# The last 96 feed-forward features computed token-major and turned by DMA, in one transformer block

## The chip, the cores and the metric

The kernel runs on one core of one Trainium2 chip. The time is the device time of a run in microseconds (us). A ratio is the mean time of one kernel's fast runs over the mean of the fast runs of the kernel before in the same rounds, so it is not quite the ratio of the medians that are quoted. "Span" is the time from the first to the last instruction in a trace. It is about 1.8 us shorter than the device time of the same run.

In profile lines PE is TensorE, PEld its loads of stationary tiles, DVE is VectorE, ACT is ScalarE, POOL is GpSimd, SP is SyncE, which here only issues DMAs; a "q" after the name means the engine's sequencer. L903 is line 903 of that kernel.

## The reference, cut to what matters

```python
h = _layernorm(x) * (1 + ca) + sa
x = x + ga * attention(h)              # 32 heads of 16, a softmax feature map, linear attention
h = _layernorm(x) * (1 + cb) + sb
g = silu(h @ w_gate); u = h @ w_up     # (2048, 512) @ (512, 1376)
x = x + gb * ((g * u) @ w_down)        # (2048, 1376) @ (1376, 512)
```

1376 features are 10 blocks of 128 and one, block 10, of 96.

## The kernel before

The program is recorded as operations with their engine alternatives. A long list, `ORDER`, made offline, says in which order a small planner takes them; the planner gives buffers and PSUM banks and so fixes each engine's instruction order. Attention for the next tokens and the feed-forward of the last ones are interleaved in it.

```python
UNITS = [(0, 0, 1), (0, 1, 1), (0, 2, 1), (0, 3, 1), (1, 0, 2), (1, 2, 2), ...]  # chunk, first tile, tiles (6 units have 2)
...
def ffn_gu(unit, ms, guT):                       # some feature blocks ms of one unit
    ...
    def f(ps_, wt):                              # features stationary, tokens moving: the result is feature-major
        for q, m in enumerate(ms):
            for k in range(KD):
                nc.tensor.matmul(ps_()[0:fsz, q * n:(q + 1) * n], lhsT=wt[:, k, m * P:m * P + fsz], rhs=h2[k], ...)
    pl.op("PE", ..., fn=lambda: f(g, wg_sb))     # gate, its own bank (L903)
    pl.op("PE", ..., fn=lambda: f(u, wu_sb))     # up, its own bank (L903)
    ...                                          # ACT: silu (L910); DVE: multiply (L913), or ACT copy + POOL multiply (L917, L919)
def ffn_down(unit, t, guT):                      # gu stationary, w_down moving (L949)
    ...
for ms in [... blocks 0 to 9 ...] + [[FM - 1]]:  # FM - 1 = 10, the block of 96, is its own group
    ffn_gu(unit, ms, guT)
```

Ones are multiplied on TensorE in some of its gaps ("fillers", L1015); their results aren't used.

The softmax here doesn't subtract the row's maximum and nothing guards it: scores larger than these inputs give would overflow.

## Time and profile before

| | before |
|---|---|
| device time, median of 3 runs | 211.17 us (210.75 to 211.92) |
| span of the trace | 208.8 us |
| TensorE clock granted | recorded as full throughout (but in the first 4 us matmuls of 512 columns start 427 ns apart, later 216 ns) |
| start of the last `phik` accumulation (end of stage one) | 56.27 us |
| start of the last matmul (end of stage two) | 205.46 us |
| fillers and idle gaps of TensorE in stage two | 0.65 and 0.59 us |

The two times in the middle cut the run into a stage that GpSimd paces and one that TensorE paces. They are read from the starts of single matmuls in the trace. The difference, 149.19 us, is the length of stage two. The page, the chain and the matmul groups are in the prediction.

### The profile page before, as it was taken

Reading aid. Unit: us, or ns where it says so; the run is one execution under the profiler, and the core shown is the slowest. Engines: PE = TensorE matmul, PEld = TensorE weight load, DVE = VectorE, ACT = ScalarE, POOL = GpSimd, SP = SyncE. Lnnn points to the kernel's source line nnn. Section 1 sums busy time; section 2 is a strip of 40 time slices with the busy share of each in tenths; the row PEclk is TensorE's granted clock in tenths of the full one; section 3 lists DMA queues with packets and bytes.
Section 4 is the critical chain, followed back from the end, with each engine's and each line's share of the span. In section 5 each row is a group of like instructions: output and inputs, shape, how many; then the busy total and the mean of one; then the engine's idle time right before and its main releaser. Section 6 shows DMA issues by size and latency. Waiting matters only on the chain.

```text
span 208.8 us, 4769 instructions
## 1 busy us (share of the span) xinstructions
PE 201.6 (97%) x1802; PEld 140.3 (67%) x1825; DVE 141.7 (68%) x337; ACT 115.3 (55%) x244; POOL 133.3 (64%) x175
## 2 busy tenths in 40 slices
PE   7899999999999999999999999999999999999994
PEld 2665564545556689779857866886875888846973
DVE  6698998999467896898789876884823431335224
ACT  2798999999798965325324721345424435410530
POOL 3358999899950558939648995587377737362230
PEclk9999999999999999999999999999999999999999
DMA  5999994994000012141311223212320010022001
GB/s 177 344 386 115 347 177 81 389 384 137 3 0 0 3 27 54 29 51 25 79 25 28 75 52 82 48 25 53 101 52 0 28 50 25 16 64 75 3 25 50
DMA packets 31465, 19.24 MB, mean 92 GB/s; under 512 B 22513, under 2 KB 28114, under 8 KB 31442
## 3 DMA queue, kind: packets, MB, share of 16 engines
q1 hardware_dynamic: 31152, 18.85, 33.6%
q8 instruction: 14, 0.23, 0.4%
q10 hardware_dynamic: 290, 0.08, 0.2%
q14 instruction: 9, 0.07, 0.1%
HBM read 11.58 MB, written 2.10 MB: 66 GB/s over the span
## 4 chain that ended last, share of the span: by engine, by line
PE 82%; ACT 8%; POOL 4%; DMA 2%; issue 2%; SPq 1%; DVE 0%; ACTq 0%
PE one_ps L903 37%; PE one_ps L949 18%; PE one_ps L849 6%; PE one_ps L670 4%; POOL phik L639 4%; PE four_ps L778 4%; PE one_ps L614 3%; ACT e L621 3%; PE one_ps L610 3%; DMA wqkv_sb<-in_A_wqkv_dram 2%; PE kv_ps L1015 2%; ACT hT L581 2%; ACT eT L676 2%; PE one_ps L444 1%; PE one_ps L489 1%
## 5 line engine op out<-in xcount | busy, mean ns | idle before, releaser
L910 ACT ACTIVATE sg<-one_ps 128x512 bf16<-128x512 f32 (+3 forms) x52 | 26.1, 528 | 46.8 <-PE one_ps L903 45.4
L903 PE MATMUL one_ps<-hT,wu_sb 128*128 128x256 bf16 (+3 forms) x440 | 45.2, 251 | 0.1
L903 PE MATMUL one_ps<-hT,wg_sb 128*128 128x256 bf16 (+3 forms) x440 | 44.8, 251 | 0.1
L903 PEld LDWEIGHTS <-wu_sb 128*128 128x128 bf16 (+1 forms) x440 | 36.8, 100 | 6.1
L949 PE MATMUL one_ps<-wd_sb,gu 128*128 128x512 bf16 (+2 forms) x168 | 40.0, 372 | 0.4
L903 PEld LDWEIGHTS <-wg_sb 128*128 128x128 bf16 (+1 forms) x440 | 36.8, 100 | 4.7 <-issue 0.2
L913 DVE TENSOR_TENSOR gu<-one_ps,sg 128x512 bf16<-128x512 f32 (+2 forms) x30 | 17.8, 596 | 24.8 <-PE one_ps L903 21.3
L919 POOL TENSOR_TENSOR gu<-usb,sg 128x512 bf16<-128x512 bf16 (+1 forms) x22 | 22.3, 1020 | 18.6 <-ACT usb L917 10.2
L639 POOL TENSOR_TENSOR phik<-e,R 128x1024 bf16<-128x1024 bf16 x16 | 30.6, 1928 | 1.6 <-ACT eT L676 0.7
L949 PEld LDWEIGHTS <-gu 128*128 128x128 bf16 (+1 forms) x187 | 17.9, 98 | 15.5
L917 ACT CAST usb<-one_ps 128x512 bf16<-128x512 f32 (+1 forms) x22 | 11.5, 523 | 21.4 <-PE one_ps L903 21.4
L381 DVE BATCH_NORM_STATS2 st<-x_c 128x6 f32<-128x512 bf16 x32 | 21.3, 681 | 1.5 <-DMA x_c<-in_A_x_dram 1.3
L836 POOL TENSOR_TENSOR o<-o 128x512 bf16<-128x512 bf16 x14 | 16.1, 1151 | 7.5 <-DVE o L816 7.5
L816 DVE TENSOR_TENSOR o<-four_ps,A 128x512 bf16<-128x512 f32 x32 | 20.6, 684 | 0.0
L631 DVE TENSOR_REDUCE S<-e 128x64 f32<-128x1024 bf16 x16 | 19.2, 1199 | 1.3 <-ACT e L621 1.0
L960 DVE TENSOR_TENSOR fg<-one_ps,gab 128x512 bf16<-128x512 f32 (+1 forms) x16 | 10.6, 672 | 12.0 <-PE one_ps L949 9.3
L676 ACT ACTIVATE eT<-one_ps 128x512 bf16<-128x512 f32 x32 | 17.7, 640 | 1.5 <-PE one_ps L670 1.4
L852 DVE TENSOR_TENSOR x_c<-x_c,one_ps 128x512 bf16<-128x512 bf16 x16 | 11.0, 685 | 10.5 <-PE one_ps L849 10.3
L621 ACT ACTIVATE e<-one_ps 128x512 bf16<-128x512 f32 x32 | 17.8, 638 | 0.0
L610 PE MATMUL one_ps<-Wk,hT 128*128 128x512 bf16 x63 | 16.3, 379 | 0.4 <-ACT hT L581 0.2
L849 PE MATMUL one_ps<-wo_sb,oT 128*128 128x512 bf16 x58 | 16.1, 379 | 0.3
L670 PE MATMUL one_ps<-hT,Wq 128*128 128x512 bf16 x62 | 15.3, 379 | 0.1
(109 smaller groups left out, 287.1 us busy)
## 6 DMA issues: line engine op xcount, KB each, us to landing
wmod_sb<-in_w_mod_dram SPq DMA_DIRECT2D x2, 1024.0 KB, 7.5
out_dram<-ot SPq DMA_DIRECT2D x15, 128.0 KB, 2.1
wg_sb<-in_B_w_gate_dram SPq DMA_DIRECT2D x1, 1376.0 KB, 8.3
wu_sb<-in_B_w_up_dram SPq DMA_DIRECT2D x1, 1376.0 KB, 11.3
wd_sb<-in_B_w_down_dram SPq DMA_DIRECT2D x1, 1280.0 KB, 14.3
x_c<-in_A_x_dram SPq DMA_DIRECT2D x4, 256.0 KB, 4.7
wmod_sb<-in_w_mod_dram SPq DMA_DIRECT2D x4, 256.0 KB, 5.3
wqkv_sb<-in_A_wqkv_dram SPq DMA_DIRECT2D x2, 512.0 KB, 6.8
```

What stands on the lines that cost most here:

```text
L381: pl.op("DVE", r=reads, w=[st6], us=0.6, fn=lambda: nc.vector.bn_stats(st6()[:], src))
L610: nc.tensor.matmul(pk()[:], lhsT=hT[c_i][k][:, cols], rhs=Wk2[:, k, :], start=(k == 0), stop=(k == KD - 1))
L621: nc.scalar.activation(e()[:, :, sg].rearrange("p g h f -> p g (h f)"), pk()[:].rearrange("p (g n) -> p g n", g=G), ACT.Exp, scale=(1.0, - ...
L639: pl.op("POOL", r=[e, R], w=[bphik[i]], us=1.92, fn=lambda: nc.gpsimd.tensor_tensor(bphik[i]()[:].rearrange("p g s h f -> p (g s h) f"), e ...
L670: nc.tensor.matmul(pq()[:], lhsT=Wq2[:, k, j * P:(j + 1) * P], rhs=hT[c_i][k][:], start=(k == 0), stop=(k == KD - 1))
L676: pl.op("ACT", r=[pq, btab], w=[beT[c_i, sg, j]], us=0.48, fn=lambda sg=sg: nc.scalar.activation(eTs[c_i, sg, j][:], pq()[:], ACT.Exp, sca ...
L816: nc.vector.tensor_tensor(o2()[:, sg].rearrange("p j (h d) -> p j h d", d=DH), ndv()[:, :, sg, 0:P].rearrange("p j (h d) -> p j h d", d=DH ...
L849: nc.tensor.matmul(a()[:], lhsT=oT()[:, j, :], rhs=wo_sb[:, j, :], start=(j == 0), stop=(j == KD - 1))
L903: nc.tensor.matmul(ps_()[0:fsz, q * n:(q + 1) * n], lhsT=wt[:, k, m * P:m * P + fsz], rhs=h2[k], start=(k == 0), stop=(k == KD - 1))
L910: pl.op("ACT", r=[g, btab], w=[sg], us=0.08 + 0.41 * L / CW, fn=lambda: nc.scalar.activation(sg()[0:fsz, 0:L], g()[0:fsz, 0:L], ACT.Silu))
L919: pl.op("POOL", r=[usb, sg], w=[gu], us=0.17 + 0.98 * L / CW, fn=lambda: nc.gpsimd.tensor_tensor(gu()[0:fsz, 0:L], usb()[0:fsz, 0:L], sg() ...
L949: nc.tensor.matmul(fp()[:], lhsT=b()[0:fsz, c0:c0 + P], rhs=wd_[0:fsz, m, wcs], start=(m == 0), stop=(m == FM - 1))
```

## The change

Block 10 costs TensorE as much as a full block when its 96 features are the stationary side. The change makes the 128 tokens stationary and moves the 96 features past them, so that only 96 columns are paid. The result is then token-major; the down projection needs it feature-major, so each token tile's block goes through a DMA transpose. `ORDER` was made anew.

```diff
+    def ffn_tail(unit, guT):
+        c_i, t0, w = unit
+        cs = slice((FM - 1) * P, F)
+        gu = sb("qf", "gu", [P, CW], BF16)
+        for q in range(w):
+            ps_ = bank("gu", (P, 2 * lastf))
+            ...
+                for i, wt in enumerate((wg_sb, wu_sb)):
+                    for k in range(KD):
+                        nc.tensor.matmul(ps_()[:, i * lastf:(i + 1) * lastf], lhsT=hT[c_i][k][:, toks], rhs=wt[:, k, cs], ...)
+            ...  # ACT: silu of the gate half into sgl; DVE: up half times sgl into gul[:, 0:96]
+            pl.op("XBAR", r=[gul], w=..., fn=... nc.sync.dma_start(
+                gu()[:, q * P:(q + 1) * P], gul()[:], transpose=True))
...
-        for ms in [...] + [[FM - 1]]:
+        ffn_tail(unit, guT)
+        for ms in [...]:
             ffn_gu(unit, ms, guT)
```

Cut: the new `ORDER`, four gul tiles of 128x128 whose last 32 columns are zeroed once on GpSimd, and the down projection's dependence on the turn of its own tile.

## The prediction

> **What bounds the kernel now.** I read the views in the order whole page, chain, matmul groups by shape, timeline. From the page come these lines:
>
> ```profile
> span 208.8 us, 4769 instructions
> ...
> PE 201.6 (97%) x1802; PEld 140.3 (67%) x1825; DVE 141.7 (68%) x337; ACT 115.3 (55%) x244; POOL 133.3 (64%) x175
> ...
> PEclk9999999999999999999999999999999999999999
> ...
> PE 82%; ACT 8%; POOL 4%; DMA 2%; issue 2%; SPq 1%; DVE 0%; ACTq 0%
> ```
>
> TensorE is busy nearly throughout at its full clock, and 82% of the chain that ended last is its. But busy is not the same as bound: up to about 56 us it also multiplies a tile of ones to fill gaps, and these count as busy. So I ask the chain, in order of time, where one limit gives way to another. It starts (from 33 us) with ScalarE and GpSimd:
>
> ```profile
> 51.69 0.47 issue
> 52.16 1.33 POOL phik L639
> 53.50 0.55 issue
> 54.05 1.94 POOL phik L639
> 56.03 0.43 PE kv_ps L646 x8
> ...
> 98.17 2.23 PE one_ps L903 x40
> ...
> 163.48 17.47 PE one_ps L903 x160
> ...
> 182.69 8.65 PE one_ps L949 x40
> ```
>
> The reader is to see two stages. The first, to about 56.3 us, ends when GpSimd has made the 16th `phik` (16 times 1.93 us, almost back to back from 18.8 us in the timeline). Its last accumulation on TensorE starts at 56.27 us. After that nearly every piece is TensorE's own. I checked this by summing 1/2.4 ns per moving column plus 2.5 ns over every matmul that the program has after that point: 148.6 us, of which 0.65 us is filler. From 56.27 us to the last matmul's end at 205.65 us is 149.4 us. So the second stage has only some 0.7 us in which TensorE does nothing, nearly all between 68.8 and 72 us where the feed-forward starts (a gap of 0.25 and one of 0.28 us; gaps of just 0.216 us elsewhere are records missing from the trace). In this stage, less work on TensorE means an earlier end, one for one.
>
> The changed work, the last 96 features (block 10 of 11), is in that stage, by shape:
>
> ```profile
> L903 PE MATMUL one_ps<-hT,wu_sb 128*96 128x256 bf16 x24 | 3.6, 273 | 0.0
> L903 PE MATMUL one_ps<-hT,wg_sb 128*96 128x256 bf16 x24 | 3.6, 272 | 0.0
> L903 PE MATMUL one_ps<-hT,wg_sb 128*96 128x128 bf16 x16 | 1.7, 219 | 0.1
> L903 PE MATMUL one_ps<-hT,wu_sb 128*96 128x128 bf16 x16 | 1.5, 219 | 0.1
> ```
>
> The 272 ns are a matmul's whole latency. What counts is the distance of starts. From the timeline and the chain:
>
> ```profile
> 161.15 0.60 PE L903 MATMUL one_ps<-hT,wu_sb 128*96 128x256 bf16 x4
> 161.58 0.60 PE L903 MATMUL one_ps<-hT,wg_sb 128*96 128x256 bf16 x4
> 162.02 1.25 PE L949 MATMUL one_ps<-wd_sb,gu 128*128 128x512 bf16 x5
> ...
> 85.43 0.45 PE one_ps L903 x8
> ...
> 88.06 0.50 PE four_ps L778 x8
> ...
> 26.30 0.26 PE kv_ps L646 x8
> ```
>
> Starts at 161.15, 161.58 and 162.02 us: four matmuls of 256 columns per 0.435 us, 109 ns each. Eight of 128 columns take 0.45 us (56 ns), eight of 144 take 0.50 us (62.5 ns), eight of 65 take 0.26 us (33 ns). A stationary of only 96 columns makes none of them faster: block 10 costs as much as a full block of 128 features. That is the waste which the change goes for.
>
> **What the Trainium skill says.** "TensorE: Matmul & The Clock Gate", section "Back-to-back issue gap", gives N/2.4 + 2.5 ns for a warm gap. The trace agrees at 256, 144 and 128 columns (109.2, 62.5 and 55.8 ns by the formula) and is 3 ns above it at 65 (29.6 ns). Section "LDWEIGHTS (loading the stationary operand)" of that page puts a load at P/1.2, 107 ns for 128 columns. The trace shows 98 ns for 128 columns, 123 ns for 96. But the starts are 33 ns apart with 128-column loads in the 65-column stream, so loads overlap and don't set the pace there. "DMA: Bandwidth & Descriptors", section "Rules for kernel authors", wants transposes from different queues serialized. Here all are issued from SP, before and after, so no such wait is added. The same page's section "Anatomy of one DMA — SWDGE (gpsimd) path" fits some 2.0 us of fixed cost (for another queue kind). The trace has 2.3 to 2.4 us from issue to landing of a transpose.
>
> **The change part by part.** *Removed from TensorE:* the first four units hold one token tile (8 matmuls of 128 columns), the other six hold two (8 of 256). 4 x 8 x 56 ns + 6 x 8 x 109 ns = 1.79 + 5.23 = 7.02 us.
>
> *Added to TensorE:* 16 token tiles x 8 matmuls with 128 tokens stationary and 96 features moving. No row has 96 columns. The points at 128 and 65 bracket it, and 96/2.4 + 2.5 gives 42.5 ns. I take 43 ns, an estimate from the formula and the 33 ns seen at 65. 128 x 43 ns = 5.5 us. The loads rise from 80 to 128, which costs nothing if they stay hidden. The work falls by 7.02 - 5.5 = 1.5 us. The changed program's own order of matmuls agrees: after the last accumulation it has 146.4 us without fillers, by the same sum, against 148.0.
>
> *ScalarE:* removed are 4 x 0.260, 6 x 0.376 and 6 copies x 0.361 = 5.5 us. Added are 16 silus of 96 columns, 0.23 us each (along the line through 260 ns at 128 columns and 376 at 256) = 3.7 us. *VectorE:* 4 x 0.277 us removed, 16 x 0.24 us added, +2.8 us, which lies beside TensorE: VectorE is busy 38.8 of the 45 us from 72 to 117 us and less after. *GpSimd:* six multiplications of 0.67 us go; four small memsets of about 0.13 us come early. None of these is on the second stage's path.
>
> *SP queue:* 16 more transposes. The path from a tail's last matmul to the turned block is latency of the matmul 0.2 + silu 0.23 + multiply 0.24 + transpose 2.4 + hops, say 4 to 5 us. In the changed order the closest reader (the down projection) comes 8.5 us of TensorE work after its tail, most 10 to 25 us. So it is hidden, unless SP stands behind an earlier issue.
>
> *Moved:* the whole order of the program was made anew, and this is the part that I can't read off a row. Comparing the two orders: the last `phik` of stage one still has 16 products and six normalizations in one GpSimd row ahead of it, so its length should stay. But VectorE now takes two Wk copies (0.69 us each) in place of two hT evictions (0.34 us each) just before the statistics of tiles 4 to 7, some 0.6 us later; part of that is lost in the waits that GpSimd has there today (0.6 us at 21.3 us). I book +0.2 us. At the start of the feed-forward there are four fillers instead of three, so the gap is a little longer: +0.2 us. The end (last matmul, an addition of 0.42 us, two stores) has the same form in both.
>
> Sum: 211.17 - 1.5 + 0.2 + 0.2 = 210.1. A new order made for the new program may as well have found something, so I shade it to 209.9 us.
>
> **The rivals.** (1) *The loads set the pace.* With 128 loads of 98 ns laid end to end the tail would cost 12.5 us, +5.5 us: 216.7 us. Against it stands the 65-column stream at 33 ns with the same loads. If a load's floor were 56 ns, the tail would cost 7.2 us, and the time would stay at 211.4. (2) *The turned block comes late.* SP issues in order, and it already waits up to 23.6 us for one GpSimd product; an oT transpose behind a waiting tail would delay attention. Each late one costs what exceeds the 8.5 us slack; two or three of 1 us would eat the gain: 211 to 212 us. For it: VectorE near 86% busy from 72 to 117 us. Against it: oT transposes are rarely next to a tail that isn't ready. (3) *Stage one decides.* If the changed engine choices delay or hasten the first `phik`, everything shifts by that, up to about 1 us either way: 209 to 211 us. (4) *Nothing moves* because TensorE isn't bound: ruled out by the 0.7 us of idleness.
>
> **Range and chances.** The gain on TensorE is sure to about 0.2 us. The new order's side effects are what spreads the result, about 1 us each way, and the three runs of before spread 1.2 us. I take 208.4 to 211.6 us. Faster by over 2% needs 206.9 us, 3 us beyond what the work gives: 0.04. Slower by over 2% needs 215.4 us, which only rival 1 or several late blocks would bring: 0.03.
>
> **What would show it.** Right: the 128 new matmuls start 42 to 44 ns apart, the matmuls after the 16th `phik` take about 147.5 us with gaps below 1 us, the chain stays with TensorE after 56 us, and the down projection never waits for a transpose. Wrong: starts of 56 ns or more in the tail; last `phik` off 56 us by over 0.7 us; gaps ended by gu transposes or by late hT or oT tiles in the second stage.

## The result, and the profile after

The changed kernel took 208.67 us (208.21 to 209.14, 4 runs) against 211.08 us (4 runs) of the kernel before: ratio 0.988, interval 0.984 to 0.992. It is some 1.2% faster: inside the predicted range, by less than the 2% that were called unlikely, and faster than the predicted 209.9.

The page of the changed kernel, its parts 1 and 4. The chain's share of TensorE has risen from 82 to 92%:

```profile
span 207.3 us, 4949 instructions
...
PE 202.4 (98%) x1876; PEld 140.0 (68%) x1876; DVE 143.1 (69%) x351; ACT 114.0 (55%) x244; POOL 131.0 (63%) x172
...
PE 92%; DMA 2%; ACT 1%; POOL 1%; DVE 1%; SPq 0%; issue 0%; DVEq 0%
```

TensorE's busy time is 0.8 us higher than before, though it has less to do. Busy time counts fillers, and matmul records can be missing (in stage two of the first trace 16 are, seen as gaps of just 0.216 us; in the new one none): the distance of starts is the measure. These are the new matmuls in the groups by shape (count | busy us, mean ns | idle before), then two token tiles of one unit in the timeline (start, length, what):

```profile
L948 PE MATMUL one_ps<-wg_sb,hT 128*128 128x96 bf16 x64 | 5.5, 206 | 0.0
```

```profile
158.50 0.33 PE L948 MATMUL one_ps<-wg_sb,hT 128*128 128x96 bf16 x4
158.67 0.33 PE L948 MATMUL one_ps<-wu_sb,hT 128*128 128x96 bf16 x4
...
159.18 1.03 PE L978 MATMUL one_ps<-wd_sb,gu 128*128 128x512 bf16 x4
```

Each line is four matmuls; two such lines, cut here, come between the second and the down projection at 159.18. Sixteen matmuls take 159.18 - 158.50 = 0.68 us, or 42.5 ns each, with a load of 128 columns for every one of them. Over the whole trace the median distance is 42 ns. Block 10 of a unit of two tiles took 0.87 us before.

Stage two shrank from 149.19 to 147.42 us. Here is that length in every kernel, with the end of stage one beside it:

| kernel | device time, median | ratio | last `phik` accumulation | last matmul | stage two |
|---|---|---|---|---|---|
| before | 211.08 | 1 | 56.27 | 205.46 | 149.19 |
| before_again | 211.01 (1 run) | | 56.72 | 205.91 | 149.19 |
| changed | 208.67 | 0.988 | 56.54 | 203.96 | 147.42 |
| after_again (the changed kernel) | 208.51 | 0.9891 | 55.77 | 203.19 | 147.42 |
| cols128 | 210.03 | 0.9968 | 55.77 | 204.88 | 149.11 |
| merged192 | 208.59 | 0.988 | 55.86 | 203.19 | 147.33 |
| merged192_no_late_fill | 208.41 | 0.9884 | 55.92 | 203.63 | 147.72 |
| turn_on_pe | 212.34 | 1.0061 | 57.02 | 208.25 | 151.23 |
| turn_twice_apart | 212.15 | 1.0070 | 55.49 | 206.38 | 150.90 |
| turn_twice | 224.89 | 1.064 | 55.70 | 220.74 | 165.04 |
| new_order_old_block | 214.77 | 1.0195 | 56.29 | 210.59 | 154.31 |
| old_order_fitted | 215.67 | 1.022 | 56.63 | 210.64 | 154.01 |
| old_order_in_place | 222.84 | 1.0542 | 57.07 | 216.32 | 159.25 |

The profile of turn_twice is used for the order of events and for what its clock does, not to compare times.

The first stage varies by a microsecond from run to run, the second hardly at all. Of the 1.77 us, 1.58 are columns: 7.02 us of old block 10 less 128 x 42.5 ns = 5.44 us. The other 0.2 us is at the start of the feed-forward: fillers and idle gaps of stage two sum to 0.86 + 0.17 us now, 0.65 + 0.59 before.

The prediction took the turn for hidden. It is, but look at the first one. The first fence is SP's queue in the timeline of the changed kernel (the length is the time that the issue holds the queue, its own waits included), the second the chain around the first reader:

```profile
72.31 7.41 SPq L841 DMA_TRANSPOSE oT<-o  x2
79.77 1.24 SPq L957 DMA_TRANSPOSE gu<-gul  x1
```

```profile
83.32 0.45 PE one_ps L906 x8
83.77 0.65 PE one_ps L978 x3
```

The first gul was ready at 74.14 us. SP could issue its transpose only at 79.77 us, because an oT transpose stood in front and waited for GpSimd. It landed at 83.36 us, and the stationary load of block 10 for the down projection (the third matmul of the group at 83.77) began at 83.83 us: 0.5 us to spare. A second one was as tight: its gul was ready at 128.58 us, but the transpose, behind stores and other transposes in SP's queue, was issued at 147.54 us, landed at 149.88 and was read at 150.47 us, 0.6 us later (which transpose a load waits for is read from its semaphore). The next margin is 2.2 us (landed at 94.62, read at 96.8). In this trace TensorE waits for none of them.

### The profile page after: what moved, and what is told of

It reads as the page before. It is cut to its first block, busy times and chain, and to the rows that moved or that the text cites. A ratio compares the mean times of both kernels' runs of the same rounds, so it can differ in the third digit from the quotient of the medians.

```text
span 207.3 us, 4949 instructions
## 1 busy us (share of the span) xinstructions
PE 202.4 (98%) x1876; PEld 140.0 (68%) x1876; DVE 143.1 (69%) x351; ACT 114.0 (55%) x244; POOL 131.0 (63%) x172
## 4 chain that ended last, share of the span: by engine, by line
PE 92%; DMA 2%; ACT 1%; POOL 1%; DVE 1%; SPq 0%; issue 0%; DVEq 0%
PE one_ps L906 34%; PE one_ps L978 18%; PE one_ps L852 7%; PE one_ps L613 6%; PE one_ps L673 6%; PE one_ps L617 5%; PE four_ps L781 4%; PE one_ps L948 3%; PE kv_ps L1046 2%; DMA wqkv_sb<-in_A_wqkv_dram 2%; PE kv_ps L649 2%; PE one_ps L447 1%; PE one_ps L551 1%; PE one_ps L540 1%; ACT e L624 1%; POOL phik L642 1%
## 5 line engine op out<-in xcount | busy, mean ns | idle before, releaser
L906 PE MATMUL one_ps<-hT,wg_sb 128*128 128x256 bf16 (+1 forms) x400 | 41.0, 251 | 0.0
L906 PE MATMUL one_ps<-hT,wu_sb 128*128 128x256 bf16 (+1 forms) x400 | 40.9, 251 | 0.0
L913 ACT ACTIVATE sg<-one_ps 128x512 bf16<-128x512 f32 (+1 forms) x42 | 23.7, 576 | 27.6 <-PE one_ps L906 26.4
L906 PEld LDWEIGHTS <-wg_sb 128*128 128x128 bf16 x400 | 32.7, 98 | 4.8
L906 PEld LDWEIGHTS <-wu_sb 128*128 128x128 bf16 x400 | 32.9, 98 | 4.2
L916 DVE TENSOR_TENSOR gu<-one_ps,sg 128x512 bf16<-128x512 f32 (+1 forms) x26 | 16.6, 640 | 22.1 <-PE one_ps L906 12.8
L922 POOL TENSOR_TENSOR gu<-usb,sg 128x512 bf16<-128x512 bf16 x16 | 18.5, 1155 | 16.8 <-ACT sg L913 13.3
L994 POOL TENSOR_TENSOR ot<-x_c,fg 128x512 bf16<-128x512 bf16 (+1 forms) x14 | 15.7, 1118 | 8.8 <-DVE fg L990 8.8
L990 DVE TENSOR_TENSOR fg<-one_ps,gab 128x512 bf16<-128x512 f32 (+1 forms) x16 | 10.7, 672 | 11.5 <-PE one_ps L978 10.8
L920 ACT CAST usb<-one_ps 128x512 bf16<-128x512 f32 x16 | 9.3, 586 | 16.3 <-PE one_ps L906 14.4
L617 PE MATMUL one_ps<-wqkv_sb,hT 128*128 128x512 bf16 x64 | 15.9, 379 | 0.1
```

What stands on the lines that cost most here:

```text
L617: nc.tensor.matmul(v()[:], lhsT=hT[c_i][k][:, cols], rhs=wqkv_sb[:, k, 2 * D:3 * D], start=(k == 0), stop=(k == KD - 1))
L913: pl.op("ACT", r=[g, btab], w=[sg], us=0.08 + 0.41 * L / CW, fn=lambda: nc.scalar.activation(sg()[0:fsz, 0:L], g()[0:fsz, 0:L], ACT.Silu))
L922: pl.op("POOL", r=[usb, sg], w=[gu], us=0.17 + 0.98 * L / CW, fn=lambda: nc.gpsimd.tensor_tensor(gu()[0:fsz, 0:L], usb()[0:fsz, 0:L], sg() ...
```

## The experiments

**after_again.** No edit.

> The changed kernel once more, with more rounds. The ratio of its first four runs was 0.988 (0.984 to 0.992), but the two traces differ by only 1.5 us of span (208.8 to 207.3, 0.993). Theory A (the traces tell all: 1.6 us of matmul columns, plus and minus some tenths): ratio 0.992 to 0.994. Theory B (the unprofiled runs gain something that the profiled ones don't show): ratio 0.986 to 0.990.

208.51 us (208.11 to 208.86, 6 runs), ratio 0.9891 (0.9869 to 0.9914). Theory A falls as it was written: the timed gain, 2.3 us, is more than the first two traces showed. The number is theory B's, but not its cause, since a profiled run shows the gain too. The second trace shows why: stage two is again 147.42 us, but stage one ended at 55.77 instead of 56.54 us.

**before_again.** No edit; a second trace of the kernel before.

> The kernel before once more, for a second trace of it. The changed kernel's second stage (last phik accumulation to last matmul) took 147.42 us in both of its traces, 1.77 us less than the 149.19 of the kernel before, while its first stage ended at 56.5 and at 55.8 us. Theory 'first stage varies': the second stage here is again 149.0 to 149.4 us, and the first ends anywhere from 55.8 to 57.3 us; what the timed ratio (0.989, 2.3 us) has beyond 1.8 us is then a first stage that ends earlier on average. Rival: the second stage of the kernel before varies too, and is longer here (149.8 us or more).

Stage two is 149.19 us again, stage one ended at 56.72 us. So the gain of stage two, 1.77 us, is firm, and the rest must come from stage one. Over all traces the last accumulation begins at 56.04 us on average in the nine traces with the new order (55.49 to 57.02), and at 56.67 us in the four traces with the old one (56.27 to 57.07), 0.6 us later. What differs steadily is the time from the first `phik` to the last: 34.4 to 34.5 us in the nine, 35.1 to 35.9 in the four. GpSimd's waits from 18 to 57 us, in us in total, times, longest, first before:

```profile
POOL phik L639 <- ACT eT L676: 0.7, 1, 0.7
POOL xn L431 <- PE one_ps L444: 0.6, 1, 0.6
POOL phik L639 <- DVE R L637: 0.5, 2, 0.3
POOL xn L431 <- DVE ln_nmr L417: 0.2, 1, 0.2
POOL phik L639 <- ACT va L627: 0.2, 1, 0.2
```

and in the changed kernel:

```profile
POOL phik L642 <- ACT eT L679: 0.7, 1, 0.7
POOL phik L642 <- PE kv_ps L649: 0.3, 1, 0.3
POOL xn L434 <- DVE ln_nmr L420: 0.3, 1, 0.3
POOL xn L434 <- PE kv_ps L649: 0.2, 1, 0.2
```

GpSimd has the same products and normalizations in that stretch, but waits 1.5 instead of 2.2 us. That this stretch is shorter by the new order is shown by the nine and four traces: one of the nine has the new order without the tails, two of the four have the tails without the new order. Which of its moves does it was not isolated.

The end of stage one also varies for a reason that was overlooked at first. Here are eight matmuls of 128 columns near 7.2 us (start, length), in the kernel before and in the changed kernel:

```profile
7.17 0.62 PE L537 MATMUL one_ps<-ident_b,wqkv_sb 128*128 128x128 bf16 x8 [0.53 <-DMA wqkv_sb<-in_A_wqkv_dram]
```

```profile
7.27 1.03 PE L540 MATMUL one_ps<-ident_b,wqkv_sb 128*128 128x128 bf16 x8
```

The second eight start at half pace, 107 instead of 56 ns apart, though the record grants the full clock. Half pace lasts until 8.6 to 10.7 us in four traces (before_again, changed, turn_on_pe, old_order_in_place) and ends by 7.0 us or sooner in the other nine. The four end stage one at 56.8 us on average, the nine at 56.0. So the first pair of traces set a quick start before against a slow one after, which hid part of the gain. Among quick starts the new order ends stage one 0.6 us sooner (seven traces and two), among slow ones 0.1 us (two and two). No run tests this; how much of the 0.6 us is the order's own stays open.

**cols128.** 128 moving columns where 96 are wanted, and 32 thrown away; every other instruction as in the changed kernel.

```diff
-            ps_ = bank("gu", (P, 2 * lastf))
+            ps_ = bank("gu", (P, 2 * P))
-        cs = slice((FM - 1) * P, F)
+        cs = slice(F - P, F)
```

> The changed kernel with 128 instead of 96 moving columns in each tail matmul (32 of them not used), all else alike, to the instruction. 128 matmuls at 56 instead of 42.2 ns make 1.75 us more of TensorE time. Theory 'columns, one for one': last matmul 1.6 to 1.9 us later than in the changed kernel, ratio to it 1.008. Rival 'slack' (TensorE has room in the second stage, and the gain came from elsewhere): under 0.6 us.

210.03 us (209.81 to 210.65), ratio 0.9968, which is 1.008 of the changed kernel. The two tiles seen above now begin like this in the timeline:

```profile
159.00 0.39 PE L948 MATMUL one_ps<-wu_sb,hT 128*128 128x128 bf16 x4
159.22 0.39 PE L948 MATMUL one_ps<-wg_sb,hT 128*128 128x128 bf16 x4
```

They start 0.22 us apart instead of 0.17, and stage two is 1.69 us longer. 128 x 13.3 ns (32 columns at 1/2.4 ns) is 1.71 us. Columns count one for one in stage two.

**merged192.** Gate's and up's last columns side by side in one weight tile: 64 matmuls of 192 columns instead of 128 of 96.

```diff
-                for i, wt in enumerate((wg_sb, wu_sb)):
-                    for k in range(KD):
-                        nc.tensor.matmul(ps_()[:, i * lastf:(i + 1) * lastf], lhsT=..., rhs=wt[:, k, cs], ...)
+                for k in range(KD):
+                    nc.tensor.matmul(ps_()[:], lhsT=..., rhs=wg_sb[:, k, F - lastf:F + lastf], ...)
```

> The changed kernel with the last 96 columns of w_up loaded behind w_gate's in one tile, so that a tail is 4 matmuls of 192 columns instead of 8 of 96: half the matmuls and half the loads of stationary tiles, the same columns. Theory 'columns': 64 fixed parts of 2.5 ns fewer, 0.16 us, not to be told from no change (ratio to the changed kernel 0.997 to 1.001). Rival 'loads set the pace in the tail': 64 times up to 50 ns, 1 to 3 us faster.

208.59 us (5 runs), ratio 0.988. Starts are 82 ns apart (96 columns: 42), stage two is 0.1 us shorter (the rest of the expected 0.16 us went into a wait for a turned block, see the next run). Halving the loads brings nothing else, so the loads did not set the pace. The time cannot be told from that of the changed kernel.

**merged192_no_late_fill.** The same, without the fillers before the first feed-forward unit.

```diff
-        if late and not o.news:
+        if late:
             return
```

> The merged 192-column tail, and without the four filler matmuls (0.86 us of TensorE) that stand before the first feed-forward unit. If real work is ready behind some of them, TensorE starts the feed-forward up to 0.4 us sooner: ratio to the changed kernel 0.997 to 0.999. Rival: TensorE stands there anyway until its inputs come (the chain to the first hT tiles), nothing moves; or the clock falls after the idle microsecond (then the granted clock says so, and it is slower).

208.41 us, ratio 0.9884; the granted clock is full. Stage two is 0.4 us longer than with the fillers, and the cause is not where they stood. It is a turned block that came late:

```profile
150.41 1.91 PE L982 MATMUL one_ps<-wd_sb,gu 96*128 96x512 bf16 x8 [0.32 <-DMA gu<-gul]
```

By the distance of starts TensorE stood 0.5 us here. It is the block that had 0.6 us to spare in the changed kernel; here it landed at 150.36 us (why later was not followed up). In merged192 the same block cost 0.1 us, and in turn_twice_apart, below, 0.5 us. So the turn is hidden in the changed kernel by a small margin, and not in each of its relatives.

The fillers themselves made no difference: the first tail still starts 15.2 us after the end of stage one. The chain ahead of it in this kernel says why (start, length, what):

```profile
66.31 0.70 DVE x_c L860
...
69.39 0.78 POOL xn L434
```

It is the way of the first token tile through residual, statistics and normalization. TensorE stands there for its input, with or without fillers. No version beats the changed kernel clear of noise.

**turn_on_pe.** The 16 turns by a TensorE transpose into a PSUM bank and a ScalarE copy.

```diff
-            pl.op("XBAR", r=[gul], ..., fn=... nc.sync.dma_start(gu()[...], gul()[:], transpose=True))
+            pl.op("PE", r=[gul], w=[tp], fn=... nc.tensor.transpose(tp()[:], gul()[:], ident_b[:]))
+            pl.op("ACT", r=[tp], ..., fn=... nc.scalar.copy(gu()[...], tp()[:]))
```

> The changed kernel in its own order, but the 16 tail blocks are turned by TensorE (one transpose of 128 columns each, a PSUM bank) and ScalarE (a copy of 128 columns) instead of by DMA. Theory 'columns, one for one': 16 times 56 ns = 0.9 us of TensorE more, ratio to the changed kernel 1.003 to 1.006, and more only if the extra bank makes waits. Rival 'the DMA turn costs' (SP's queue, late blocks): as fast as the changed kernel or faster.

212.34 us, ratio 1.0061, 1.7% slower than the changed kernel: above the expected 1.003 to 1.006, and against the rival. What came is the reservation, "more only if the extra bank makes waits". Of 3.8 us more in stage two, 0.9 are the columns. The other 2.9 us are new gaps; TensorE's waits name ScalarE, which empties the banks:

```profile
PE one_ps L994 <- ACT sg L959: 0.7, 1, 0.7
PE one_ps L994 <- ACT usb L966: 0.6, 1, 0.6
```

The four banks of stage two are shared by all its matmul groups. The order was not remade for this version, so 2.9 us is what it costs put in so, not the least that it can cost.

**turn_twice and turn_twice_apart.** Each transpose issued twice: into the same place, then (second try) the second into a spare tile.

```diff
-            nc.sync.dma_start(gu()[:, q * P:(q + 1) * P], gul()[:], transpose=True)
+            [nc.sync.dma_start(dst, gul()[:], transpose=True) for dst in (gu()[:, q * P:(q + 1) * P], spare[gul.slot][:])]
```

> The changed kernel with each of its 16 DMA turns issued twice, into the same place. In the trace of the changed kernel each holds SP's queue 1.1 to 1.2 us and lands 2.3 us after issue. Theory 'hidden': the turned block is needed so late that another 1.2 us each is absorbed; ratio to the changed kernel 0.999 to 1.003. Rival 'SP's queue is nearly full where the first tails stand' (there an oT, the next attention tile's, stands behind): 0.5 to 3 us slower, with waits of TensorE for oT or raw tiles.

> As turn_twice, but the second transpose of each tail goes to a spare tile. In turn_twice (224.9 us) the second one of each pair waited in SP's queue until the first had landed, so that SP was held 3.4 us longer per tail, not 1.1. Here only the issue itself, 1.1 us, is doubled: 16 x 1.1 = 18 us more of SP's queue in some 110 us. Theory 'hidden with room': 208.3 to 209.5 us. Rival 'SP's queue is the next bound': at least 0.3 us per tail appears, 213 us or more, with TensorE waiting for oT, raw or gu tiles.

224.89 us and 212.15 us. The first was not the test that I meant: the second write to the same place waited in SP's queue until the first had landed (78.93 issued, 82.44 the next), so that SP was held 3.4 us longer for this first tail and 2.2 to 2.3 us for each of the others (the 3.4 us per tail of the second expectation was read from the first alone). The clean version adds 1.2 us each, 16 x 1.2 = 19 us of SP's queue, and costs 3.5 us of stage two: neither theory's number, between the two. TensorE's waits in it:

```profile
PE one_ps L853 <- DMA oT<-o: 1.2, 2, 0.9
PE one_ps L907 <- ACT hT L878: 0.5, 1, 0.5
PE one_ps L979 <- DMA gu<-gul: 0.3, 1, 0.3
```

Mostly it is not the turned block that is late, but the attention's oT and the next hT (whose raw tile comes by a transpose too), which stand behind it. SP's in-order queue is a limit close behind TensorE. With the 16 transposes of the changed kernel it is full enough that another 16 cost something, and not yet so full that the present ones do: stage two has 0.17 us of gaps.

turn_twice showed one thing more. TensorE's longest wait there ends in this line of the timeline; below it is the stretch after it, from the view by windows (busy time and count of each engine, then the granted clock, here 0.72):

```profile
161.52 2.95 PE L978 MATMUL one_ps<-wd_sb,gu 96*128 96x512 bf16 x8 [3.56 <-DMA gu<-gul]
```

```profile
160.00:166.00 6.00, 4.48 (x18) 2.35 (x19) 1.48 (x3) 0.00 (x0) 1.03 (x3) 0.72 0.21 60
```

The late block cost more than its wait: from 162.2 to 165.6 us, 3.4 us long, matmuls started at twice the usual distance (427 ns for 512 columns).

**new_order_old_block.** The new order with block 10 computed feature-major in the tail's place.

```diff
-        ffn_tail(unit, guT)
+        ffn_gu(unit, [FM - 1], guT)     # where ORDER has the tail
```

> The order of the changed kernel, but with block 10 computed the old way, features stationary, where the tail stood. TensorE's real work in the second stage is again 148.0 us. Theory 'columns' (the gain is the 1.6 us of matmul time): last matmul some 1.6 to 2.2 us later than in the changed kernel, ratio to the kernel before 0.998 to 1.003. Rival 'order' (the newly made order brings the gain by itself): ratio 0.99 or below.

214.77 us, ratio 1.0195 (1.017 to 1.0221): slower even than the kernel before, by more than either theory said. That the new order brings the gain of stage two by itself is not borne out. But the plain theory is not right either: TensorE's work is again that of before, and 5.1 us of stage two came on top, as gaps (5.1 us in all, 0.6 before) and fillers (1.3 us, 0.65 before). The longest waits:

```profile
PE one_ps L884 <- DMA oT<-o: 1.8, 1, 1.8
PE one_ps L1015 <- POOL gu L954: 0.8, 1, 0.8
```

In the trace a block-10 product (0.67 us, at 127.16 us, after 2.6 us of waiting for its input) stands on GpSimd ahead of the product `o` at 129.11 us, of which the late oT is made. So this run shows what the old block costs in that place, and not the order's share of stage two by itself.

**old_order_in_place and old_order_fitted.** The old order with tails. In the first the four parts of a tail follow each other where block 10 stood; in the second they stand at the head of the unit, each part where its engine is free anyway by the planner's reckoning.

```diff
-ORDER = [ ...new... ]
+ORDER = [ ...old, without block 10... ]   # tails taken in at its place / at the unit's first group
```

> The order of the kernel before, with each block 10 replaced by the token-major tails at its place; nothing else moved. TensorE's work falls by the same 1.6 us. Theory 'columns, one for one' in its plain form: as fast as the changed kernel, ratio 0.992 to 0.995. Rival 'the order had to be made anew' (around the first feed-forward units another engine is nearly as full, so that TensorE saved there only waits; the program's own order has 3.0 us more of filler matmuls there, and two tails have only about 5 us before their reader): no gain or a loss, ratio 0.998 to 1.01, with gaps or fillers of 1.5 to 3 us between 75 and 86 us.

> The order of the kernel before again, but the tails stand at the head of each unit, and each of their ScalarE, VectorE and SP parts is put where its engine would come to it without standing still. In old_order_in_place (222.8 us) these parts stood right behind the matmuls, and VectorE stood idle 2.3 to 2.5 us before several of them. Theory 'it was the place of the small operations in the in-order queues': most of the 12 us loss goes, 209 to 212 us. Rival 'SP': each extra transpose holds SP's queue 1.1 us wherever it stands, and delays oT; still 214 us or more, with waits for oT.

222.84 and 215.67 us. The loss is far above what I expected of the first: its gaps and fillers in stage two sum to 12.9 us beside 146.4 us of work (1.0 us in the changed kernel), and not only between 75 and 86 us. Fitting the small operations took away 7 of the 12 us: more than half, but short of the 209 to 212 us expected. What is left (7.6 us of gaps and fillers) has this as its largest entry among TensorE's waits:

```profile
PE one_ps L952 <- DVE gul L1000: 1.9, 3, 0.6
```

A tail holds a bank for only 0.34 us of matmuls, but until silu and product are done; the next group, given the same bank, waits. The gap after three of the tails is 0.79 us each time. Rival 'SP' is a smaller part: 0.7 us for oT in the second version, 2.1 in the first. So for this order, taken as it was, the cheaper block is a loss. Both versions are my insertions; how well an old order can be patched with more care stays open.

## Why the prediction was right or wrong, point by point

- *The second stage is TensorE's, one for one.* Right. The planned test of it, cols128, gave 1.69 us for 1.71 us of columns, and stage two took 147.4 us where about 147.5 were forecast.
- *"The work falls by 7.02 - 5.5 = 1.5 us."* Right, and 0.08 us too small: the pitch is 42.5 ns, not the 43 taken.
- *"I book +0.2 us" for the first stage, whose "length should stay".* This step failed, in its sign. I compared the counts of operations on GpSimd, which are equal, and saw only that VectorE comes later to some statistics. The first `phik` did come 0.3 us later on average (19.42 us in nine traces, 19.08 in the two of the kernel before), but the length did not stay: from the first `phik` to the last it fell from 35.4 to 34.4 us on average, and stage one ended 0.6 us earlier (part of which may be the uneven starts told above). "Almost back to back" was a loose reading: of the 37.2 us of GpSimd's row 30.8 are `phik`, the rest six normalizations, one more product and waits for other engines, and an order can change the waits.
- *"At the start of the feed-forward ... +0.2 us."* Wrong in sign too. A fourth filler was there, but the idle gaps around fell from 0.59 to 0.17 us: a filler takes the place of a wait that is there in any case.
- *The sum, 210.1, shaded to 209.9.* The two failed terms (0.2 for -0.6, 0.2 for -0.2) are 1.2 us, just what separates the sum from a gain of 2.3 to 2.4 us. The shade of 0.2 us was a guess that went the right way. The mechanism was right, the side effects of the order were mis-sized. They had been given 1 us each way, and the range held.
- *"the closest reader (the down projection) comes 8.5 us of TensorE work after its tail"*. Right for the program's order, but it gave a false margin: the first block waited 5.6 us in SP's queue and came 0.5 us ahead of its reader, another waited 19 us and came 0.6 us ahead. The reservation "unless SP stands behind an earlier issue" was the actual case for it.
- *Rival 1 (loads)* is out: 42 ns with a load each, and merged192. *Rival 2 (late blocks)* did not happen in the changed kernel, but it was near: in merged192_no_late_fill one block came 0.5 us late. *Rival 3 (stage one decides)* happened in part, to the good. (Two small slips: VectorE's sum is +2.7 us, not +2.8, and rival 1 with a floor of 56 ns gives 211.3 us, not 211.4; nothing hangs on them.)

## What to carry to other kernels

When a block is narrower than the array, put the narrow side on the moving operand: columns are what TensorE is paid in, and in a stage that it bounds they count one for one. The gain comes only with an instruction order that fits: here the same cheaper block under the old order, or the new order under the old block, were each slower than the kernel before. Before adding DMA transposes, count the time that they hold the issuing queue and what stands behind them, not only how long they take to land.

## What the Trainium skill lacked or had wrong

- "TensorE: Matmul & The Clock Gate", section "Back-to-back issue gap": it gives about 81 ns at 128 columns and 131 ns at 512 for streams in which each matmul has its load, and calls N/2.4 + 2.5 the isolated case. Here streams with a load for each matmul run at 42 ns (96 columns), 56 (128), 109 (256) and 216 (512). The formula fits them; the other figures don't.
- The same page, section "LDWEIGHTS (loading the stationary operand)": by P/1.2 a load of 96 columns is shorter than one of 128. Here it took 123 against 98 ns. (Section "Weight-path perf modes — Fast Weight Load (FWL) and DoubleRow" says that the fast load needs 128 weights, which goes with this.) Neither sets the pace: matmuls of 128 moving columns start 56 ns apart with both.
- The same page, section "Why this matters for your kernels": it asks for no pauses over some 3 us between matmuls. In turn_twice pauses of 3.7 us and, later, of 2.6 us were each followed by matmuls at twice the distance (213 instead of 109 ns at 256 columns), the granted clock being half for 3.4 us each time. One of 2.3 us, in old_order_in_place, was not.
- "DMA: Bandwidth & Descriptors" has no figure for how long the issue of a small transpose from SBUF to SBUF holds its queue on this chip (its part on trn3 gives cycles for other cases). Here it is 1.1 to 1.2 us, hardly less for 128x128 (median 1.18) than for 128x512 (1.20 to 1.22), and it lands 2.3 to 2.4 us after issue. On a queue with 44 transposes (14 of oT, 14 of raw tiles, 16 of gu) and 16 stores in 150 us, 16 more cost 3.5 us (turn_twice_apart).
